# A recurrent attention and soft mixture-of-experts kernel: 24 pieces of unread products on TensorE, and a new table of order

## The chip, the cores and the metric

The kernel runs on one core of a Trainium2 chip. The metric is the time of the program on the device in microseconds (us), as the median of several runs. One run was also recorded by the hardware profiler; the rows below come from that run. The engines are called PE (TensorE: matmuls and transposes), DVE (VectorE), ACT (ScalarE), POOL (GpSimd) and SP (SyncE, which here issues the DMAs). PE's weight loads are listed apart as PEld.

## The reference

The first half is a recurrence over 768 tokens for 4 batches and 8 heads of dimension 40, the second a soft mixture of 8 experts with 4 slots each over its output:

```python
for t in range(S):                                   # S = 768, state is D x D = 40 x 40 per batch and head
    y[:, :, t] = np.einsum('bhd,bhde->bhe', rt, state)
    Sa = np.einsum('bhde,bhe->bhd', state, at)
    state_decay = state * wt[:, :, None, :] - np.einsum('bhd,bhe->bhde', Sa, bt)
    state = state_decay + np.einsum('bhd,bhe->bhde', vt, kt)
...
logits = x @ phi                                     # x: 3072 x 320 (the y of above), 32 slots
d = softmax of logits over the 3072 tokens;  slot_input = d.T @ x
h = np.maximum(slot_input[e] @ w1[e], 0.0);  slot_out[e] = h @ w2[e]     # e of 8, 320 -> 1024 -> 320
c = softmax of logits over the 32 slots;     return c @ slot_out
```

## The kernel before

The recurrence is cut into 12 steps (`st`) of 64 tokens, two to a superstage. Inside a step all tokens are solved at once. `scan_s`, `scan_c` and `scan_k` form running products of the decay on DVE and scale the inputs by them, `bda_at` spreads them, and `gram` multiplies them with each other on PE. `solve_half` (superstage 0) and `solve_step` (the later ones) invert the resulting triangular matrices row by row on DVE and POOL, for a whole superstage; `solve_out` brings the inverse into the layout that PE needs, with a stream transpose on DVE. `ctok_of` and `kbtok` are transposes on PE of scaled inputs.

What runs from step to step is `chain(st)`, in two quarters q of 32 tokens: `chain_v` (products with the values, 32 small matmuls of 32x40), `chain_a` (with the state of before), `chain_e` (a copy), `chain_u` (the nested function `times`: 32 products with the inverse; steps 0 and 1 run it three times, with copies between), and at the end `chain_s`, which forms the new state. `y_ut`, `y_sd`, `y_p` and `y_y` make the output of a step one step later, and `slots` gathers the expert slots. Behind the last step stand `merge_m` and `merge_s` (which bring the partial slots together), the experts' two layers, and 16 output blocks with a DMA each.

All of it is recorded first. Every call of an engine goes through the class `Plan`, which collects operations; an operation is what one stretch of code records for one engine. `emit` then prints them in the order that the string `ORDER` gives (two characters are the number of an operation). The string `ENGINE` chooses DVE or ACT, or DVE or POOL, for each operation that may run on either, and `BANKS` the PSUM bank of each temporary. So each engine's instructions run in the order of the table, and an instruction waits only for what it reads, what it overwrites and its place in its engine's row. The profile gives one line (L509) for all of them, since they are printed by one helper; they are told apart by operation and tile. `cs_t` is the tile of the constants (128x227): `ident`, the unit matrix, its first 128 columns, and some masks. DMAs are all issued by SP in the order of the table.

An f32 matmul call is two matmuls and two weight loads on PE in the trace, a transpose or an f32r matmul one of each.

Of the kernel before, what the change touches and what calls it, by code (L numbers as in the profile page):

```python
# [32 lines left out]


ORDER = (
    "#,#-#/#0#.#2#1#7#4#5#6#3#(#+#&#$#%#9#8#;#:#<#=#@#>#B$R$P#?#D#C#A#'$V#I#H#K#J#G#L#M#F#N$S#E$W$T#e$Q#X#Y#Z#]#["
    "#^#_#P$U#T#g#Q$X#f#O#i#j#`#o#R#n#U$h$_#W#V$e#S$g#h$j$Y$i$`$l#s#m#y#p#q$n$k#{#c$m$o$(#b#k#r$q#a#t#z$#$)#l$*%3"
    "$%$p#d$$$t$M#v#u$N$u$r%2$c$''B$s&O$-$d$x$w$v$&$a&P$.&A$b%5&B$]#w$1$^$f$2$3$Z#}$[&;%4$4%8%7$5&I%6'G#x&C$6$7&J"
    "$+$8$9%9$:%:$;$<%<$,&<%=$y&=%#&E&>%>%-()%;%?$=%@%A%(%,(*$>$?&F%*$0$@${#|$|%&$z%''E%G$A$B$C$D$E$F$G&D$}%0%$$H"
    "$/$I$J$K$L$O%L('%)((%O#*&N%B%F%I%Q%R&Q&R%+&S%%%M&T%/&U%E%C%N&V&Y&W&r&q&s&n&o&p&t&u&w&X%D&Z&y&v&[%K%1&G'=&]'F"  # L40
    "%T&^%H%S%.'@&z&x&{&|%U%V(2%P&_'%'H%W'I%Y%J'#&H&`'D){&a&b%Z&}%[%]%^%_%`%a%b&g)y%c'J&c&e&d'L'$(4'>&f&j&l)|&h'K"
    "&k&m'?'w&i'('M'C's'&''(1'O'P'q(3%d'Q'R(5%e(7'8'S)E%f(6'x)z'.'T'<%X'N%g%h't%i'))@#)'3'r%j':'9%k'/%l'U'W'V%m'A"
    "'Y(9'X'u%n)F'y(<';'Z%o'+'p%p(8'-(U)>%q%r'2%s%t%u%v&K'0'6(;(=+1'v'*+/'[(-(:)A'z'{','1(?'5(@(/(>(++0(F)B'4']'7"
    "(K+2)I'|(P(0(H%w(.'^%x'_%y%z%{%|%}&#&$(,&%(G*((#&&&''}(&(%($&((M(J(O(L)G&)'`(I'a&?)J)H(S*$(N(A'd'e'c'b'f'g&*"
    "*)&+&,'m&-&.&@&/)C*+)<*-&0(Q**&1&2'j(D'h'n(C)D)K'i&3&4&M'k'o)h)j(R'l*,)=)M*Q&5)L&6&7&8&9(B)?(E)n*.)N)i)k)p&:"
    "*&(V(W(X)O(Z)l(T*V)S*P)Q)P&L)T)g)o)R*Z)q)U)r)V)m*0*/*L*4([(](^(_)W*3)}*1)v*'*N*X)s*W*2+e*[+_+b*%*R(`(a(b(c*6"
    "*5*7*=(d(e+`*8+c*S)[)Z)Y(f(g)X)]*#*Y(h(i(j*9(k(l(m)u*?+a+d)^)d)a+f(n*B*>)_*T+g*O*F)e*A)`)b*])f)c*^*_(o(p(q(r"
    "*;)x*C*`*U*a)t)w*<*@*:*y*f+i+h*{(s*E(t(u*D+9+$(v+&+j(w(x(y+k*z*|+^+;*}*c*d*b*e*g,m+3*h*G,i+%*I(z+:+m*M*H({+>"
    "+?+#+<*i+**K+'*l+(*k*j*m,n,k+7,j,l+5*r*n+4+l+,(|(},g)#*u*x)$)%+=+6)&+n+o*o*J,h)'+A)())+8+D+@)*+s+B+E,o+p+C(Y"
    "+G+F+H)+*v+q.R.S*s),)-).*w.T-A-B*t-C-D+S+W+I+).U,e-G+U*p+N*q)/+M+X)0)1)2,f,`,p,b+++t+T)3-K)4)5)6+Z,r+.)7+R,q"  # L50
    "+L-M)8-P-0-8,d+K+P+V+Y+J+O)9):);+z,s-1,w,v,u,t,x-6-2+{+-,y-v+Q+|-E,z-I-w-7-3,{-L+u,c-4-/-N+]-O+[,a-Q-|.#-5-9"
    "-#,},|-$-%-)->-:.$,#,$,%.%,&,',(,),*,+,,-F+r-*-J-=-},-,.-,-x-;-&-H,/-z,0,1/',2,3/*+}-+/----y.X/(/)-<-.-@-'-("
    ".&/+-p/..(/,,4-R//.)-S,5-U.A-V.C-{/1.+.'-W/2-T.-.*-r,6.,.//3../=/4,7,8-q-?/0.I.^,9.G.B,:.D.E.0,;.]/6-s-Y-Z-X"
    ".1.M0/,<.`.O,=.c.H.F-[/5,>.J.Q.2,?.6.Z,@.4.V.b.3.5._,A-t03/7,B-u.a-^.N,C.d,D,E.K00.g-].Y.f-a04.=0501.L,F-c.e"
    ".[.7-`.>.?06-k.W-_02-f.:/<0U.8.@.i,G-l.h.9-m-i07,H,I,J,K,L,M,N0i-o.;-n.<0g.j.k1x0V/8-e.l/>0j-b1y.w/&.P,O,P,Q"
    ",R,S,T,U,V,W,X.m-j09-g0:080;/91:-h.r0+0h.z.|0<0W.p.n0*.t0T/:,Y.q-d.s.v0q,Z,[,].o.y0^0[0s0v,^,_/D.x0=0X0Y/#.}"
    "/E/F/H/I/J.{1F0A0@0>0?0C0B0Z0]1z0o1H.u0k0_/G1@0D1?/K/L/$0.1{/%/M1A0E0r0G0F0t0,0H0`0w1D0m0I1>0a2K1I0d0N1E0Q0p"
    "0J1B2N1=/N2L1G0K2Q1C/O/P/Q2M2O2P1J0l2R/;0-0n2S0b/R2T0u/S0x/T0y0c0f1g/U0z0|0{0L0R/V0O/W1i0M1m5K1#0S0P1K0}1%1L"
    "1h1$150e1M1N2U1o/X/Y/Z/[/]/^1;1j2V1k/_2W/`/a2X2b172(2Z16/b1O1Q1S2'1P1R1T1U2Y/c/d2*1n1&2[181(101V1l2)191p/e/f"
    "1'122+/g2./h2//i1*/j/k142,/l/m1q2a/n1[1)1f1+/o/p/q1<2-2#211r1Z111Y5J1X3Q22201W46131c1]231w262$/r25244,3R1d1e"  # L60
    "3O4.1`1^1_2F3P1|274-4/2<1-2A1}/s/t1a1b3Y/u1.3Z/v/w/x3[2I/y/z/{2c2%1u2H2:2D2?2J2;/|/}1,0#2G2B3W293]1/3U5Y1s28"
    "3S400$0%2&0&0'0(0)3X2i2=2C2@2>1t3x2j2k2m2n2o4#3^3V2p2q3|3}472E3_3b3`3v3y3a3d3c4A42482]5A3w5@3e1v2^3T4{4y3u2_"
    "4G2r2s2t2u2v2w2x3f4B4|3z4I3{2y4z443g3k3i3j3h4C4D5T/@3o3N3r4@4=4$4%4H2z2{2|2}3s3#3t4K3$5D3l3p414&3q4}5h5%435&"
    "5(3m3n3%4L3&3'4M5#4N5B5$4O5C5[5Z4E5E3(494(3)4J4)3*4'4+4h454F4n3+4S5)3,4j3-4R3.4p3/30314P4Q4U4T4V5'325X5*4W33"
    "342l354k365M5G4i375L38393:3;3<5V5F5W4*4l5,4o3=5`3>3?4m3@4q4Y4X4Z4[4d4a4]5b2`4^4e4;5-5.3A4b4g5/3B5c4f4<5U4r5j"
    "5+/?5_506D4c5a3C5d5f3D3E5^4_3F4`3G3H3I3J3K3L3M5g5?5]4:4t4v5l5k5m4u4x635i6-51525n5e6+585s+v+w+x+y4s616B5o6.53"
    "5N625I6,745p5r5q6<2e2f2g2h5t5u575v5S5H54556@5x59/A5R4w6//B5z5y605w5|64/C565;6$656E6%6&6'7?6*666m6C6A6=5}6F6("
    "6j6p6n6k6)6#757A5{6>706l6H6G6q6I5P6o6r6J6L6?6N6M4>68696K675<5O6;5=6X6Z6a6P6O6_6Y4?7,6[6t6:6]6u6Q6v6w7C6s6x6`"
    "6b7=76797:6c7D7G7f6R7B6^6d7W##7@7i6{6W7^7;7m2d6|777-5Q6U6}6e7<6S6g7E7Z6f6i7Q7[7M7>6y7e7R6h6T7k7X7K7H7S7N7L7O"
    "7Y5:6z7$7T7_7U7%7]7`7P7V7u7#7x8(7{7y8)7/7g7&5>7v7w7|7z7}8$8%8#8&7I738-8.7q8'837'7.8K8L7r8/72878*8889848?807p"  # L70
    "818A8>7l828B7c8,718M8C8@8D8E8F8G858I8H8J8N8O8P8Y8Z7d8Q8[8]8j8X8S8W8T8V8U8i6V8k8R8x7(7)7*7+8y788c7s868^8:7j8r"
    "8d7h7a7o7t8;8s7b8_8a8f8l8e8m7n8g8h8b8z8w8t8v8`8u8n8o8p8q9>8<9?9@9A8{8=9B9L9F9R9X8+7F7J9Y9G9I9H9O8|9M9U9C9Z9N"
    "9S9J9K9T9P9Q8}9#9$9V9%9,9W9)9*9D9&9'9E9-9.95929698939/9+999094919(979:9;9<9="
)
# [1163 lines left out]
```

## Time and profile before

| what | value |
|---|---|
| median of 3 runs | 364.82 us (363.41 to 366.78) |
| the profiled run's own time | 365.54 us |
| its span in the trace | 363.7 us |
| PE busy | 322.2 us, 89% of the span, 7425 matmuls |
| DVE busy | 287.4 us, 79% |
| ACT busy | 225.4 us, 62% |
| POOL busy | 115.6 us, 32% |
| mean granted clock of PE | 0.961 |

The profiled run's time is that of the whole program and the span that of what the profiler shows inside it; 1.8 us lie around the span. Busy time is a share over stages with different limits, so the stretches and the chain of waits say more than this table. The granted clock of 1.0 is 2.4 GHz, 0.5 is 1.2 GHz.

### The profile page before, as it was taken

Reading aid. Unit: us, or ns where it says so; the run is one execution under the profiler, and the core shown is the slowest. Engines: PE = TensorE matmul, PEld = TensorE weight load, DVE = VectorE, ACT = ScalarE, POOL = GpSimd, SP = SyncE. Lnnn points to the kernel's source line nnn. Section 1 sums busy time; section 2 is a strip of 40 time slices with the busy share of each in tenths; the row PEclk is TensorE's granted clock in tenths of the full one; section 3 lists DMA queues with packets and bytes.
Section 4 is the critical chain, followed back from the end, with each engine's and each line's share of the span. In section 5 each row is a group of like instructions: output and inputs, shape, how many; then the busy total and the mean of one; then the engine's idle time right before and its main releaser. Section 6 shows DMA issues by size and latency. Waiting matters only on the chain.

```text
span 363.7 us, 16917 instructions
## 1 busy us (share of the span) xinstructions
PE 322.2 (89%) x7425; PEld 281.5 (77%) x7425; DVE 287.4 (79%) x608; ACT 225.4 (62%) x527; POOL 115.6 (32%) x230
## 2 busy tenths in 40 slices
...
GB/s 245 337 248 16 241 14 159 84 51 191 35 172 205 62 77 194 196 87 77 262 104 187 195 99 203 260 205 167 187 235 230 168 295 108 268 313 250 3 192 243
DMA packets 35938, 62.42 MB, mean 172 GB/s; under 512 B 3832, under 2 KB 21368, under 8 KB 35864
## 3 DMA queue, kind: packets, MB, share of 16 engines
...
q8 instruction: 58, 0.95, 1.1%
...
## 4 chain that ended last, share of the span: by engine, by line
PE 72%; DVE 12%; issue 6%; POOL 4%; ACT 2%; DMA 1%; DVEq 0%; ACTq 0%; POOLq 0%
PE ps L509 72%; DVE wt L509 8%; POOL wt L509 4%; DVE ps L509 3%; ACT wt L509 2%; DMA wt<-in_aa_dram 1%; DVE mem L509 1%; ACT mem L509 0%; ACT old_r L509 0%; ACT mid_r L509 0%; DVE slx L509 0%; DVE old L509 0%; POOL mem L509 0%; DVE mlast L509 0%; ACT mid L509 0%
## 5 line engine op out<-in xcount | busy, mean ns | idle before, releaser
L509 PE MATMUL ps<-wt,wt 32*32 32x40 f32 (+7 forms) x2936 | 143.4, 239 | 10.5 <-issue 5.3
L509 PEld LDWEIGHTS ps<-wt,wt 32*32 32x32 f32 (+7 forms) x2936 | 131.1, 133 | 19.5 <-issue 10.2
L509 PE MATMUL ps<-wt,mem 128*64 128x40 f32 (+7 forms) x1088 | 88.0, 295 | 2.7 <-issue 2.3
L509 ACT ACTIVATE wt<-ps 32x320 f32<-32x320 f32 (+1 forms) x181 | 72.8, 402 | 19.6 <-PE ps L509 13.6
L509 PEld LDWEIGHTS ps<-wt,mem 128*32 128x32 f32 (+6 forms) x1088 | 67.3, 123 | 16.0 <-issue 9.8
L509 ACT COPY wt<-ps 32x256 f32<-32x256 f32 (+4 forms) x126 | 55.7, 458 | 18.9 <-PE ps L509 8.6
L509 POOL TENSOR_TENSOR wt<-wt 128x220 f32<-128x220 f32 (+17 forms) x107 | 49.4, 462 | 50.8 <-DVE wt L509 30.2
L509 POOL TENSOR_TENSOR wt<-wt,wt 128x108 f32<-128x108 f32 (+16 forms) x97 | 48.9, 504 | 40.2 <-DVE wt L509 31.9
L509 ACT COPY mem<-ps 128x320 f32<-128x320 f32 (+4 forms) x79 | 32.5, 430 | 46.5 <-PE ps L509 44.0
L509 PE MATMUL ps<-cs_t,wt 120*128 120x120 f32 (+4 forms) x352 | 46.7, 274 | 15.7 <-DMA cs_t<-in_consts_dram 10.0
L509 DVE TENSOR_TENSOR wt<-ps,cs_t 64x512 f32<-64x512 f32 (+1 forms) x74 | 49.3, 677 | 5.1 <-PE ps L509 4.8
L509 PEld LDWEIGHTS ps<-cs_t,wt 120*128 120x128 f32 (+4 forms) x352 | 37.5, 147 | 18.4 <-ACT wt L509 15.8
L509 PE MATMUL ps<-wt 120*64 120x192 f32 (+1 forms) x288 | 47.3, 314 | 0.0
L509 DVE TENSOR_TENSOR_SCAN ps<-wt,wt 128x390 f32<-128x390 f32 x48 | 45.5, 966 | 0.3
L509 PEld LDWEIGHTS ps<-wt 120*64 120x64 f32 (+1 forms) x288 | 36.4, 137 | 0.0
L509 DVE TENSOR_TENSOR wt<-wt,ps 128x384 f32<-128x384 f32 (+1 forms) x48 | 34.4, 740 | 0.6 <-ACT wt L509 0.5
L509 ACT ACTIVATE wt<-wt,bm_t 128x768 f32<-128x768 f32 (+1 forms) x36 | 29.1, 867 | 3.1 <-DVE wt L509 3.1
L509 DVE TENSOR_TENSOR wt<-wt,wt 128x234 f32<-128x234 f32 (+15 forms) x67 | 21.7, 324 | 5.0 <-POOL wt L509 3.6
L509 POOL TENSOR_SCALAR_AFFINE_SELECT wt<-wt 128x1024 f32<-128x1024 f32 x6 | 7.6, 1266 | 56.1 <-DVE wt L509 41.9
L509 DVE STREAM_TRANSPOSE wt<-wt 128x1024 f32<-128x1024 f32 x12 | 24.7, 2081 | 0.7 <-ACT wt L509 0.3
L509 PEld LDWEIGHTS ps<-mem,wt 32*32 32x32 f32 x1792 | 19.4, 108 | 6.3 <-ACT mem L509 3.3
L509 PE MATMUL ps<-mem,wt 32*32 32x40 f32 x1792 | 22.9, 201 | 1.4 <-ACT mem L509 0.5
...
## 6 DMA issues: line engine op xcount, KB each, us to landing
...
```

Of the source, the lines that this page charges most:

```text
L509: eng.dma_start(dst, src)
```

## The change

A new function records 24 pieces. Each is two f32 products of the unit matrix with the whole tile of constants, into a PSUM bank of its own that no operation reads. The tables are replaced by others, in which the pieces have their places. Of the tables one line of each is shown.

```diff
@@ -33,47 +33,48 @@
 ORDER = (
-    "#,#-#/#0#.#2#1#7#4#5#6#3#(#+#&#$#%#9#8#;#:#<#=#@#>#B$R$P#?#D#C#A#'$V#I#H#K#J#G#L#M#F#N$S#E$W$T#e$Q#X#Y#Z#]#["
...
+    "#(#,#-#&#7#1#0#/#.#2#3#5#6#$#%#Q#P#?#S#R#4#T#V#U#Y#W#@#Z#'#B#X#`#8$k#q#]$i#[#a#_#b$m#^$l$o#c$p#}#d#x#r#l$n$q"
...
-ENGINE = "11111111111111111111111111111111111000001100111110100000...
+ENGINE = "11111111111111111111111111111111110000111000000000001000...
-BANKS = "102327013457241654366050002150265737503402171131375156103716...
+BANKS = "700016625067633671105412104336041735637252402551000245602414...
@@ -951,6 +952,16 @@
             load_g(kbr.put(st), kb[st])
             load_g(ahs.put(st), aa[st])
         load(cs_t, consts)
+
+        def keep_busy():
+
+            v = bank("busy")
+            for _ in range(2):
+                nc.tensor.matmul(v[:, 0:227], ident, cs_t, start=True, stop=True)
+
+        for _ in range(24):
+            keep_busy()
+            nc.open = None
         for st in range(2):
             scan_s(st)
             scan_c(st)
```

On PE the number of recorded matmul calls goes from 4011 to 4059. Of the 24 pieces 13 stand ahead of the first product of the recurrence, chain_v(0,0): four at the very start, four behind the Grams of step 0, two behind those of step 1, and three single ones. One stands in `merge_s`, ten behind the last product of the program. Among the operations with a choice, `solve_half` has 8 going from POOL to DVE and 3 the other way, `solve_step` 53 from DVE to POOL and 56 back, `chain_u` 7 of its copies from ACT to DVE and 5 back, the output copies 8 from ACT to DVE and 2 back.

The start of SP's row, where the inputs of the first two steps are loaded. In before:

```order
L509 DMA wt_70<-in_ww_dram 128x782
L509 DMA bm_t<-in_consts_dram 128x3
L509 DMA wt_70<-in_kb_dram 128x768
L509 DMA wt_74<-in_aa_dram 128x384
L509 DMA wt_70<-in_kb_dram 128x768
L509 DMA wt_70<-in_ww_dram 128x782
L509 DMA wt_74<-in_aa_dram 128x384
L509 DMA cs_t<-in_consts_dram 128x227
```

In the change:

```order
L942 DMA wt_70<-in_ww_dram 128x782
L942 DMA bm_t<-in_consts_dram 128x3
L942 DMA cs_t<-in_consts_dram 128x227
L942 DMA wt_74<-in_aa_dram 128x384 x2
L942 DMA wt_70<-in_kb_dram 128x768 x2
L942 DMA wt_70<-in_ww_dram 128x782
```

The constants have moved from the eighth place to the third; the first kb load has two aa loads and the constants ahead of it instead of none.

PE, at the end of step 0's chain, from the last `times` (mem, wt_74) of quarter 1 to the state products of `chain_s` (wt_76 with wt_75); cs_t with mid is the transposes of `y_ut(0,1)`, wt_76 with wt_71, wt_72 and wt_74 is `chain_v(1,0)`, eight times the same three rows. In before:

```order
L509 MATMUL ps_62<-mem,wt_74 32x40 x32
L509 MATMUL ps_61<-cs_t,wt_73 128x120 x2
L509 MATMUL ps_61<-cs_t,wt_73 128x80
L509 MATMUL ps_63<-cs_t,mid 120x128 x3
L509 MATMUL ps_65<-wt_76,wt_71 32x40
...
L509 MATMUL ps_68<-wt_76,wt_75 120x120 x4
L509 MATMUL ps_62<-wt_76,wt_75 80x80 x4
L509 MATMUL ps_64<-wt_76,wt_75 120x120 x4
```

In the change:

```order
L942 MATMUL ps_67<-mem,wt_74 32x40 x32
L942 MATMUL ps_66<-cs_t,wt_73 128x120 x2
L942 MATMUL ps_66<-cs_t,wt_73 128x80
...
L942 MATMUL ps_68<-wt_76,wt_75 120x120 x4
L942 MATMUL ps_67<-wt_76,wt_75 80x80 x4
L942 MATMUL ps_62<-wt_76,wt_75 120x120 x4
L942 MATMUL ps_61<-cs_t,mid 120x128 x3
L942 MATMUL ps_65<-wt_76,wt_71 32x40
```

The state products have moved ahead of `y_ut(0,1)` and `chain_v(1,0)`.

PE in step 8, quarter 1, from the last products of `chain_v` (wt_76 with wt_71) to `times` (mem, wt_74); the rows between are transposes for the output, for `kbtok` and for `ctok_of`. In before:

```order
L509 MATMUL ps_61<-wt_76,wt_71 32x40 x2
L509 MATMUL ps_66<-cs_t,mid 120x128 x3
L509 MATMUL ps_67<-cs_t,wt_70 128x120 x4
L509 MATMUL ps_64<-cs_t,mem 128x128
L509 MATMUL ps_68<-cs_t,wt_73 128x120 x2
L509 MATMUL ps_68<-cs_t,wt_73 128x80
L509 MATMUL ps_62<-cs_t,wt_73 128x120 x2
L509 MATMUL ps_62<-cs_t,wt_73 128x80
L509 MATMUL ps_61<-cs_t,wt_76 120x120 x4
L509 MATMUL ps_64<-mem,wt_74 32x40 x32
```

In the change:

```order
L942 MATMUL ps_64<-wt_76,wt_71 32x40 x2
L942 MATMUL ps_65<-cs_t,mem 128x128
L942 MATMUL ps_63<-cs_t,mid 120x128 x3
L942 MATMUL ps_66<-cs_t,wt_70 128x80 x4
L942 MATMUL ps_61<-mem,wt_74 32x40 x32
L942 MATMUL ps_64<-cs_t,wt_70 128x120 x4
```

Fewer transposes stand between the two groups of small products.

## Rows read from the trace of the kernel before

**Rows 1.** The page's list of engines: busy us (share), matmuls or instructions.

```profile
PE 322.2 (89%) x7425; PEld 281.5 (77%) x7425; DVE 287.4 (79%) x608; ACT 225.4 (62%) x527; POOL 115.6 (32%) x230
```

**Rows 2.** Stretches: busy us per engine (count), granted clock, DMA share, GB/s.

```profile
0.00:10.00 10.00, 0.00 (x0) 0.02 (x1) 6.30 (x12) 2.24 (x3) 3.65 (x7) 1.00 0.78 259
20.00:30.00 10.00, 4.71 (x34) 4.36 (x33) 9.98 (x16) 9.68 (x25) 0.00 (x0) 0.92 0.55 181
...
50.00:60.00 10.00, 6.99 (x272) 5.66 (x272) 9.82 (x16) 7.93 (x20) 0.99 (x1) 0.79 0.46 143
...
70.00:80.00 10.00, 10.00 (x305) 8.99 (x296) 9.83 (x22) 7.20 (x19) 4.26 (x9) 1.00 0.21 56
```

**Rows 3.** Chain of waits: start, us, what; behind x, matmuls.

```profile
98.81 2.12 DVE wt L509
...
101.06 50.57 PE ps L509 x1336
...
234.93 3.40 PE ps L509 x127
238.33 1.07 issue
239.40 4.56 PE ps L509 x127
243.96 1.57 issue
```

**Rows 4.** Stretches at half the granted clock, same columns.

```profile
52.40:55.80 3.40, 3.40 (x102) 2.58 (x93) 3.30 (x6) 2.79 (x8) 0.00 (x0) 0.50 0.35 80
...
59.20:66.10 6.90, 5.31 (x85) 4.76 (x86) 2.85 (x8) 4.89 (x9) 3.74 (x9) 0.51 0.07 25
...
247.00:250.40 3.40, 3.40 (x25) 3.26 (x25) 1.25 (x4) 0.48 (x1) 0.54 (x1) 0.51 0.33 119
```

**Rows 5.** Timeline of PE, 10 to 40: start, us, operation, wait ahead.

```profile
10.01 3.03 PE L509 MATMUL ps<-cs_t,wt 120*128 120x120 f32 x14 [10.01 <-DMA cs_t<-in_consts_dram]
14.53 2.04 PE L509 MATMUL ps<-wt,wt 120*128 120x192 f32 x6 [1.48 <-ACT wt L509]
...
21.50 3.76 PE L509 MATMUL ps<-wt,wt 120*128 120x192 f32 x24 [0.82 <-ACT wt L509]
...
36.70 1.15 PE L509 MATMUL ps<-wt,wt 120*128 120x192 f32 x6 [0.41 <-ACT wt L509]
```

**Rows 6.** PE's waits from 62 to 360: total us, times, longest.

```profile
PE ps L509 <- issue: 8.7, 9, 1.6
```

**Rows 7.** The page's list of DMA queues: packets, MB, share.

```profile
q8 instruction: 58, 0.95, 1.1%
```

**Rows 8.** Timeline of DVE, 0 to 13 and 56 to 69.

```profile
8.87 2.73 DVE L509 TENSOR_TENSOR wt<-wt,ps 128x384 f32<-128x384 f32 x4
...
61.68 0.25 DVE L509 TENSOR_TENSOR wt<-wt 128x84 f32<-128x84 f32 x1 [1.31 <-POOL wt L509]
...
65.06 0.66 DVE L509 TENSOR_TENSOR wt<-ps,mem 120x480 f32<-120x480 f32 x1 [2.32 <-PE ps L509]
```

**Rows 9.** Timeline of PE, 56 to 69.

```profile
57.49 0.50 PE L509 MATMUL ps<-cs_t,wt 120*128 120x120 f32 x3 [1.05 <-ACT wt L509]
57.92 0.79 PE L509 MATMUL ps<-mem,wt 32*32 32x40 f32 x64
...
62.52 4.47 PE L509 MATMUL ps<-wt,wt 32*32 32x40 f32 x47 [1.32 <-issue]
```

**Rows 10.** Timeline of PE, the last matmul.

```profile
355.86 0.27 PE L509 MATMUL ps<-mid_r,mid_r 128*128 128x160 f32 x1
```

**Rows 11.** Timeline of SyncE, from 353.

```profile
354.88 4.82 SPq L509 DMA_DIRECT2D out_dram<-wt  x7
```

**Rows 12.** SyncE's waits, from 340: total us, times, longest.

```profile
SPq L1234 <- DMA out_dram<-wt: 2.9, 1, 2.9
```

More of the change, by code (lines that the diff above doesn't have):

```diff
@@ L35 @@
 ORDER = (
-    "#,#-#/#0#.#2#1#7#4#5#6#3#(#+#&#$#%#9#8#;#:#<#=#@#>#B$R$P#?#D#C#A#'$V#I#H#K#J#G#L#M#F#N$S#E$W$T#e$Q#X#Y#Z#]#["
[L37 to L70, printed above, removed]
@@ L76 @@
-BANKS = "102327013457241654366050002150265737503402171131375156103716576670522421452065361244107267553310451473165617605137503720671732071540316753612143041312053071203434532545632740110555017116264555664270243574170570701510252036710267336013643321513170435504770253352577404346014552556227605501331264612371653340752506303513552261461555075044510755166173436347747124523744344711215606351262517751262657304033277532524547652271574457175442564125463077277243105"
+    "#(#,#-#&#7#1#0#/#.#2#3#5#6#$#%#Q#P#?#S#R#4#T#V#U#Y#W#@#Z#'#B#X#`#8$k#q#]$i#[#a#_#b$m#^$l$o#c$p#}#d#x#r#l$n$q"
@@ new lines @@
+    "$$#e#t$&#f#i$j#|$'#y#g$r$,#h'/#A#j#m$+$#$(#o#s%'%%$/#k%&#p#{%($-$*%)#=$%#n#u#D%*$.#>%,$0%-$1#z#v$)$2$;%.%+$?"
+    "$w$=$<$@%0%2$6$x$B%/$3$7$}$8#9$A%1#*$:#+%J%K$E$F$I$J#;$K$u'0$v%L${$L$|%#%O$5$M$s#:$t$>%3%4%M%P$y$z&[&S&T$D$4"
+    "%5#C%N&Y&U&b&^%6$C&Z$N',$G$O%;&]%Q$f&_%$$P%R$Q&c$R%E%T$g&V%>%V&`#<%U(A#w&h$S%S$T$U$V$W&g%:$X$Y$Z$[$]$^%7%8#)"
+    "%Y%@&a%X%W%e%=(B$_$`$a%<$9$H$b$c$d'^%A'.%?%B'-$e$h%I%`%a%j&i%l%Z%9&j%i%c&k&l%g%G&m'Y%D%F%[(=&n&q&o&r&p&t%f&u"
+    "%b'X%d&s&v&w'[%k%C'2&x%H'a'7'4%^%]&y'1'3&z'5%h'9'='U'8':';'V%_&}'W'#&|%o%p&{'<'$*8*6*7(?%r''(@')'_'%'c'+'6(I"
@@ new lines @@
+    "(N'b%m'e'(%n'*'&'f'd'Z(4(0'h'i(.']*9'>'?'j'@'k(6%s%t%u%v'l'm'o'r'n%w%x%y%z%{%|%}'p(K&#(J'P'F##'Q&$(O&%'`&&(1"
+    "&''A(L(-(M&((/(2(:'q(5&)&*(Q&+(;&,&-&.&/(P&0'g'J's'T'G&1&2&3&4(R(U&5&6'D'H(T(7(3&7'K(C'B(S(G'C(E'E'S'O%q't(W"
+    "(>(X(V'R(8(n(F'u'N)^(d(H)`(D(_'M'L'v'w&8(f)U)_&W'x)a'y(Y'I&X)T(9(i&9&:&;&<&=*@(<)Y&>&?&@&A*B(b)b)V*E(e'|'z'}"
+    "'{(*&B&C(h(#)Z(Z(g&e&f&D*A&E)c)[)](+('(a&F&G&H(k&I($&J&K&L&M&N&O&P&Q&R(m*C(,(](`(c*F(((l)d*'*%([(%(&()*+*-(^"
+    ")f*&)e+G+I)g(j(o)h*(*)*<+J)X+H*D)m*k*>)l(p)k(q)i)j)n*,*.*/*l)o*H)p(s*e*G)W*L*:*K*I*=*o*0*$(t*q**+}+z*N*O*M(u"
@@ new lines @@
+    "*J*;+w*p)t*U)q)s)u)r(v(w(x(y(z&d({(|*s+{+x*P(})#)$)%)&*m*5*2+y*?*1*g*n+|*4*u,#,$)|*t*r*S)'+Q*h)y*Z*j*T*R,&,%"
+    ")(*X,',(*Q)v*i)}*W*_)z*#))*Y)*)+),){)w)-)x*3+8+6*v*x+S,**w*[*y).*{*z*}*|+#)/)0+9*f+V*]*V+<+>+$,)+M*`,++K+%+7"
+    ")1)2+:*^*b)3+R+v)4,0)5)6+=+&+W*a+T+U+X)7+Z+?+@*d+[+*,})8)9+;+)+'+():+Y+5);++*c)<+]+O,{+A,1)=+,)>+B+D+F+C+E+`"
+    "+2-#+^-(+/,|+_-))?)@.k)A)B)C+P)D)E+N+3+0+L+4-*+a.l-,)F)G-&-'-Y-Z-[-]+b-$.m+g+-+f.n+l+.+1)H---.-+)I-d-%-P-H-/"
+    "-G)J,x)K+p)L+h)M)N)O+m+q+e+d+i+c.;+k-f(r-i)P)Q)R)S,7-0+n+j+r+o+s,y,8,9,;-2,<-J-N-4-K-1-3-5-6-7,,.3-O,--`,.,="
@@ new lines @@
+    "-8,>,:,?-^-I+u.9.4+t-L-e-9-<-;-=-:,@,z,/-A,A-g-j-h,B-Q,C,D,E-M-D-R.=-B,F-C->-a-S/E/?-E-_.7.<.:/B.5/@,G/A/C,H"
+    ",I,J-F-?-@.>.?,K/D,L/F/G.1.--l.8.@-p.v-k.A-b0F,M.6/I/J/K/H/P/L-m,N,O/Q-c-o/N/R-X-U-T-V.[.].Y.Z-W.b.`.x.^./.E"
+    ".C.B.F.D.G-n-r/U/M-s-q/O.(,P,Q,R,S.H.u.s-t,T.w.y,U.2.{-v._0G0H...X.),V0K-x.z.I,W.0.a,X.c,Y,Z,[-u.K.M.J.|.d-y"
+    ".L,].N-w.e.o/#,^0L,_.t,`,a/$0O.p.U.}0P,b/>.q,c.r.R/%.,.#/&-{.O.V0I.S.+25.T0E/)0M,d-}.*.W1(0Q,e,f,g,h.P.Q/T0J"
+    ",i,j,k,l,m.i.h.f.g.j,n0R/(/',o1W0N//.%/0/3/90T,p,q,r,s,t,u,v,w26/*/4.&-|/1/V/2.'/./50n-z/-0p/,/8/+0t.$/]0U/;"
@@ new lines @@
+    "0S/60o0q0r0v/:0W0X0Z/^0u1&0s/_0V0Y1$0[/a/=/b0w0x0D1'1/110B1.1%100]12/c/d0^/e1)1*/f/</g1,0y0m/71+2g2d/h0_1]0b"
+    "0`0a0c2h0C1-141U2j1V0j1X2e0d1^1Z2f2i130k0l1Y/i/j/k/l1[1c2k2l27/m1_16150g,219/n1R/o1:/p2n1`/S172o2p/q1#0{0|0z"
+    "2&2$/r0}2q280e1;5c2*180f0h4N0i1d1e/s/t1<1=2m1f/u/v1g/`1i1l2r1a1b1M2,1O2%2'1N1k1h2(1T1j1m/w2?1Q1>/x2A/y2+2s1n"
+    "2t/z1B/{2@1H1?/|2B2C/}292)0#2-1P2.1@2G0$2F0%2K0&0'2z1A1o2J1L0(0)2I1J2/1S1I2D2#2E3r2H2y2{0*0+1C561K57214F2=1r"
+    "1p1s1q0,0-0.0/00010203042:05060708090:581x1t2;4G4D202L1F2M0;0<2<1{1y591z1u1|4E1v5d3n2N2>1G1E3o2O1}2T2Y2_3p2P"
@@ new lines @@
+    "1w1D2Q3h243j2R3s2V2b2[223q3i3t2a3k5Y452]2W3u4;0=2^0>0?2Z0@0A3&23432`3v2S2U3'492c2X3x3w444H3l3z3y3{4P3|2u5r4O"
+    "5o4Y4:4L463(5m3)3*3+3}4#3,5X4U3-4Z3.3g3/4(3m4&4'4J4%4$2v2w4`30313233343536374[38474)484<4]424/2x4,5n4d4*4041"
+    "4=4-4+394.4e4g3:3;3<3=4I3>4>5@5:4h5;4M5=4^4b5]3?3@3A3B3C3D3E5<5>5^4f4l5Z5t5[4K5w5s4A4?4@5?4C5%4c5'4Q4i4k4j3F"
+    "3G3H3I3J3K3L4X4n5&5e4o5+3M5-4_4p5A3N3O5B4m5q5x4u5(5z6%5_5,3P4S3Q5f5$3R5D4t6'5`4B4a5)3S3T3U3V3W3X3Y3Z4r/W4s3["
+    "4q4v5{5E4y5*5F4R5G4T4|3]5y5H3^3_3`3a3b3c5.5/5g5p5v5u4w6&4z5P51534{525C556K6E5I4}5#4x6(6)3d3e3f5W5J5O6*6+6I5Q"
```

15 lines of the change are left out of this document (11 added, 4 removed).

## The prediction

> **What bounds the kernel now.** I read the page first, then the stretches of ten microseconds, the chain of waits, PE's own waits, and last the timelines of the start and the end. All sums are made against the profiled execution: a span of 363.7 us and a time of 365.54 us, which is 0.7 us above the median of the three runs (364.82).
>
> PE is busy in 89% of the span [rows 1]. The stretches say where it is the bound. From 50 to 60 DVE is busy for 9.82 of 10 us and PE for 6.99: the prologue belongs to DVE. From 70 to 80 PE is full (10.00) with DVE close behind (9.83) [rows 2]. The chain of waits agrees: at 98.81 a DVE transpose of 2.12 us releases 50.57 us of PE without a break [rows 3]. So the two engines are tied together at each superstage's inverse ("solve_out"), and a change must shorten both, or one of these hand-overs.
>
> Two losses of PE can be seen. The first is its clock. In 52.4 to 55.8, 59.2 to 66.1 and 247 to 250.4 the granted clock is 0.50 or 0.51, the lower of its two levels (1.2 of 2.4 GHz) [rows 4]; a second late stretch, from 274.3 to 277.7, is like that from 247. At the start the page's clock row is no witness: six Gram products last 2.04 us at 14.53 and 1.15 us at 36.70, so the start too runs low [rows 5].
>
> The second is "issue": PE waits for nothing that the profile shows, 8.7 us in 9 pieces from 62 on [rows 6]. In the chain such pieces stand behind groups of exactly 127 matmuls (3.40 us, then 1.07 lost; 4.56, then 1.57) [rows 3]. The queue for instructions brought 58 packets, 0.95 MB, or 16.4 KB each [rows 7]; PE's 7425 matmuls and as many weight loads are 14,850 instructions, 256 to a packet, so a packet is 128 matmuls. I read it so: where PE runs through one block too quickly, the next isn't there yet.
>
> **The change, part by part.**
>
> *The pieces.* A piece is two f32 products of 227 columns, four passes over PE. 24 Gram matmuls (4096 columns) take 3.76 us at 21.50 [rows 5], so 0.92 ns a column, and 908 columns cost 0.83 us; at the low clock about 1.6 (2.04/1.15 times as much gives 1.5, and the transposes from 10.01, 3.03 us for 1600 columns, give 1.7).
>
> Four pieces stand first: 6 to 7 us at the low clock. They need only the constants, whose load moves from the eighth DMA to the third. In the first 10 us the queue moved 259 GB/s [rows 2], so the 0.51 MB up to it take 2.0 us, and with as much for the start of the queue they land near 4 us, and the pieces end between 10 and 13. PE's first real work started at 10.01, released by these constants, and its next at 14.53 waited for ACT [rows 5]. The chain from 10 to 14 is DVE and ACT, not PE. Cost 0; without ACT's lag it would be up to 2.5 us of PE, which DVE's prologue still covers. The loads that the constants pass (a kb half, 0.49 MB later) would land about 1.5 us later, near 6.5, and their first product on DVE starts at 8.87 [rows 8]: 0.
>
> The other nine pieces of the prologue (7.5 us at full clock, 15 at low) lie behind the Grams of st 0 and 1. PE idles 5.29 of the 10 us from 20 [rows 2], the largest hole; at the low clock the pieces fill it and what smaller ones there are. Cost between 0 and 1 us.
>
> *The end of the prologue.* Before, PE runs y_ut(0,1) and the 32 products of chain_v(1,0) ahead of the state products chain_s0; there it loses 1.32 us to issue, and 4.47 us pass over the next group of 32x40 products and the state products recorded with it [rows 9]. DVE waits 2.32 us there, until 65.06 [rows 8]. The change puts the state products first. They can come some 2 us earlier; but DVE's work ahead of the first inverse is the same to 0.2 us, and DVE waited 1.31 for POOL just before [rows 8]. I take a gain of a third, 0.7, with bounds of -2.0 (the whole) and +1.0 (the fillers delay a Gram).
>
> *The blocks.* Behind 62 us PE's work stands in nearly the same order (no landmark moves by more than some 4 us of work, and DVE's sum ahead of the inverses by -1.5 to +2.9 us), but cut otherwise into 256s. I summed PE's full-clock time in each block by the order and the lengths in the trace. Before, four blocks hold under 3.35 us of work (3.32, 2.99, 2.94, 2.58), and the stops behind three of them are 0.61, 1.07 [rows 3] and 0.77: 2.45 over four, 0.6 each. After, eight are so short, three of them near 2.1 us, because chain_v(st,1) and "times" of the same step now meet in a block. In step 8 they bring 60 of its calls, or 120 of 128 matmuls; 64 such matmuls take 0.79 us [rows 9], so 1.5 us, and the transposes between them bring it to 2.1. Four more at 0.6 are 2.4 us; I take half, 1.2, since several end where the chain of one quarter waits for copies anyway. Bounds: 0 (all there), and 5.6 (each costs 1.0, worked out below).
>
> The Trainium skill ("Runtime: NRT & Kernel Launch", section "Instruction fetch mechanics") describes instruction memory as refilled in 16 KiB blocks of 256 instructions, and says that this is hidden by the pace of issue. The size agrees with the 16.4 KB here; the hiding doesn't, with 8.7 us of stops. By that rule this term is 0 and the sum 0.5 above before.
>
> *The merge.* One piece, 0.83 us, between two products, where PE has a wait for DVE's small steps. 0, at most 0.8.
>
> *The tail.* Ten pieces stand behind the last product, which ended at 356.13 (355.86 + 0.27) [rows 10]. Ten are 8.3 us by the Grams, so PE ends at 364.4. Before, the last outputs left SyncE's queue in the 4.82 us from 354.88 [rows 11], to 359.70; with 2.9 us of waiting for their landing [rows 12] that is 362.6, and 1.1 us of closing steps lead to 363.7. PE becomes the last. Bounds: 0 (its columns pass a tenth quicker than the Grams', and the closing steps don't follow it) and 1.8 (364.4 and the closing steps, 365.5). I take 1.2, nearer the upper end, since the closing steps have to stand behind every engine. At the low clock it would be some 8 more, which I leave to the slower case, as PE doesn't idle ahead of it.
>
> *Copies between engines* (10 output copies, 12 of chain_u, solve steps 53 to POOL, 56 from it): equal in number both ways; ±1, taken as 0.
>
> Sum: -0.7 + 1.2 + 1.2 = +1.7, so 367.2 against 365.5; less 0.7 for the profiled run, **366.5 us**.
>
> **Rivals.** One per cent here is 3.6 us: 361.2 to 368.5 is no change.
>
> *Faster, 359.6.* If PE is occupied in the prologue, the clock is high when the chain of st 0 comes, and the low stretches go. 59.2 to 66.1 holds 5.31 us of PE at 0.51: 2.6 us too many, 2.3 of it on the path; the two late stretches hold 3.40 each, 1.7 too many each [rows 4]. -2.3 - 3.4 - 0.7 + 1.2 = -5.2: 360.3, less 0.7. For it: the waits ahead of low stretches are there to be filled. Against: the pieces stand behind the Grams and ahead of chain_v(0,0), none behind the first "times", where waits as that of 1.05 us at 57.49 stand [rows 9]; none before 247 or 274. The Trainium skill ("TensorE: Matmul & The Clock Gate", "Why this matters for your kernels") advises to leave no long idle gap between bursts, which is this rival; the trace agrees in that the low stretch from 59.2 follows such a wait, the 1.05 us at 57.49 [rows 9]. By the rule alone I would say faster.
>
> *Slower, 370.9.* A block stops PE by what it lacks of 3.35 us. The four of before lack 1.6 together and cost 2.45; the eight of after (3.31, 2.08, 3.25, 2.56, 3.02, 2.08, 2.94, 2.18) lack 5.4, which in proportion is 8.3; at 1.0 each I take 8.0, +5.6, and -0.7 + 5.6 + 1.2 = +6.1: 371.6, less 0.7. It decides if a stop costs above 0.75 on average. For it: 1.57 and 1.07 have been seen [rows 3]. Against: a block of 2.99 cost nothing before.
>
> *The pieces and the cuts do nothing, 364.8.* PE's stops stay where the chain waits anyway, its end isn't waited for, DVE's own work holds the prologue: every term is 0.
>
> Chances: forecast 0.28, nothing 0.12, faster 0.27 and another 0.05 for gains of the new order that I don't see, slower 0.24 and another 0.04 for a late clock or fillers that delay a Gram. So faster by over 1% 0.32, within 1% 0.40, slower 0.28. Signs are mixed, so the range is wide: 358.5 (faster, a good microsecond below its price) to 372.5 (the slower case with the upper bound of the tail). The forecast's own is 363.5 to 369.
>
> **What would show it.** PE's "issue" from 62 on: near 10 us for the forecast, 14 for the slower case, under 9 for "nothing". The granted clock in 52 to 66: still 0.5 for the forecast, 1.0 for the faster case. PE's last instruction near 364 and behind the last output's landing. DVE's wait ahead of the state products below 2.3 us, and the first "times" of st 2 less than 1 us earlier than 101.06. I am wrong if solve_out(0) moves by more than 2 us or if the low stretches late in the span go.

## The result

The change runs in 368.45 us (median of 20 runs, 365.53 to 374.33) against 364.63 us before (20 runs, 359.18 to 370.16): 3.8 us more by the medians. The ratio is 1.0146, with a 95% interval of 1.0112 to 1.0181. That is slower by over 1%, which had a chance of 0.28; it is inside the forecast's range, between its point (366.5) and its slower rival (370.9).

Runs of these two kernels spread over 9 and 11 us. Ratios and their intervals leave out runs more than 1.5% above the fastest of their kernel, in some sets most of before's, so medians and differences below are of all runs. Before was run again with each set of experiments: 364.14 us with e1 to e4, 364.11 with e5 to e8, 365.31 with e9 to e11. The change's profiled run took 366.61 us; only three of its 20 runs are lower, so its trace shows less of the loss than a typical run has. Its span is 364.9 us.

The page and PE's waits, which answer to [rows 1], [rows 7] and [rows 6]:

```profile
PE 335.3 (92%) x7521; PEld 295.4 (81%) x7521; DVE 295.1 (81%) x622; ACT 222.6 (61%) x521; POOL 112.6 (31%) x222
...
q8 instruction: 59, 0.97, 1.1%
```

```profile
PE ps L942 <- issue: 10.0, 10, 2.6
```

PE is busier by 13.1 us, which is less than the 22.5 us of the pieces: the other products took 9 us less, at least in part by the clock (the first Grams, below). The stops rise from 8.7 to 10.0 us behind 62; ahead of it they rise more, as the chain of waits shows (start, us, what; answers to [rows 3]):

```profile
55.69 2.44 issue
58.13 3.25 PE ps L942 x123
...
250.28 4.16 PE ps L942 x128
254.44 1.48 issue
...
264.55 3.96 PE ps L942 x126
268.50 2.61 issue
271.11 15.47 PE ps L942 x379
```

The stop at 55.69 stands inside one `times` of step 0. Stops of 0.3 us and more sum to 13.8 us over the whole span, 8.7 before. Again they come behind 126 to 128 matmuls, but for one of 0.58 us at 45.92, which stands ahead of the same product wherever the cuts fall. And something follows a stop that I had read past in the rows of before: the clock. The stretches at half (answer to [rows 4]):

```profile
50.50:64.00 13.50, 8.96 (x270) 7.49 (x271) 9.80 (x13) 7.32 (x20) 2.45 (x6) 0.50 0.39 88
...
272.30:275.70 3.40, 3.40 (x23) 3.15 (x23) 2.92 (x7) 0.19 (x1) 0.63 (x3) 0.50 0.40 111
```

The stop of 2.61 us ends at 271.11, and from 272.3 on PE runs at half for 3.40 us. In before the stop of 1.57 from 243.96 [rows 3] stands ahead of the low stretch from 247 [rows 4] in the same way. So a long stop can be paid twice. It is not always: behind the 1.48 us from 254.44 the clock stayed full.

The start and the end of PE (timeline: start, us, operation, wait ahead; answers to [rows 5] and [rows 10]) and SyncE's last waits (to [rows 12]):

```profile
4.78 5.64 PE L942 MATMUL ps<-cs_t 128*128 128x227 f32 x16 [4.78 <-DMA cs_t<-in_consts_dram]
...
13.13 2.00 PE L942 MATMUL ps<-wt,wt 120*128 120x192 f32 x12 [0.90 <-ACT wt L942]
...
17.04 3.38 PE L942 MATMUL ps<-cs_t 128*128 128x227 f32 x16
...
355.81 0.49 PE L942 MATMUL ps<-mid_r,old_r 128*128 128x160 f32 x3
356.14 7.87 PE L942 MATMUL ps<-cs_t 128*128 128x227 f32 x40
```

```profile
SPq L1245 <- DMA out_dram<-wt: 2.7, 1, 2.7
...
SPq L1245 <- PE ps L942: 0.2, 1, 0.2
```

The first four pieces last 5.64 us; the first twelve of their 16 products stand 0.38 us apart, the rest 0.19, so three quarters of them run at the low clock. The Grams behind them take 2.00 us for twelve matmuls, in before 2.04 for six [rows 5]. The last ten pieces end at 364.01 and SyncE waits 0.2 us for them behind the last output.

### The profile page after: what moved, and what is told of

Same layout as the page of the kernel before. It is cut to its first block, busy times and chain, and to the rows that moved or that the text cites. A ratio compares the mean times of both kernels' runs of the same rounds, so it can differ in the third digit from the quotient of the medians.

```text
span 364.9 us, 17101 instructions
## 1 busy us (share of the span) xinstructions
PE 335.3 (92%) x7521; PEld 295.4 (81%) x7521; DVE 295.1 (81%) x622; ACT 222.6 (61%) x521; POOL 112.6 (31%) x222
## 4 chain that ended last, share of the span: by engine, by line
PE 79%; DVE 7%; ACT 5%; issue 5%; DMA 2%; POOL 1%; DVEq 0%; SPq 0%; ACTq 0%; POOLq 0%
PE ps L942 79%; ACT wt L942 4%; DVE wt L942 4%; DVE ps L942 3%; DMA wt<-in_vv_dram 1%; DMA wt<-in_aa_dram 1%; POOL wt L942 1%; DVE mem L942 0%; ACT mem L942 0%; ACT mid_r L942 0%; ACT old_r L942 0%; DVE slx L942 0%; DVE old L942 0%; ACT mid L942 0%; ACT old L942 0%
## 5 line engine op out<-in xcount | busy, mean ns | idle before, releaser
L942 PE MATMUL ps<-wt,wt 96*32 96x40 f32 (+7 forms) x2936 | 138.5, 234 | 6.7 <-ACT wt L942 5.2
L942 PEld LDWEIGHTS ps<-wt,wt 96*32 96x32 f32 (+7 forms) x2936 | 126.7, 129 | 17.2 <-issue 7.8
L942 PE MATMUL ps<-wt,mem 128*64 128x40 f32 (+7 forms) x1088 | 86.0, 294 | 2.8 <-issue 2.6
L942 ACT ACTIVATE wt<-ps 32x256 f32<-32x256 f32 (+1 forms) x181 | 72.7, 402 | 15.9 <-PE ps L942 12.7
L942 ACT COPY wt<-ps 32x256 f32<-32x256 f32 (+4 forms) x121 | 53.2, 458 | 23.2 <-PE ps L942 12.4
L942 POOL TENSOR_TENSOR wt<-wt,wt 128x84 f32<-128x84 f32 (+16 forms) x98 | 49.2, 502 | 55.6 <-DVE wt L942 31.4
L942 POOL TENSOR_TENSOR wt<-wt 128x30 f32<-128x30 f32 (+17 forms) x98 | 46.2, 472 | 38.8 <-DVE wt L942 22.0
L942 PE MATMUL ps<-cs_t,wt 120*128 120x120 f32 (+4 forms) x352 | 44.7, 262 | 2.9 <-issue 1.6
L942 PE MATMUL ps<-cs_t 128*128 128x227 f32 x96 | 22.5, 389 | 4.9 <-DMA cs_t<-in_consts_dram 4.8
L942 DVE TENSOR_TENSOR wt<-wt 128x168 f32<-128x168 f32 (+16 forms) x66 | 22.3, 338 | 2.9 <-POOL wt L942 1.5
```

The source lines that it names most:

```text
L942: nc.gpsimd.memset(t, 0.0)
```

## The experiments

In these, *lack* is a number that the order and the matmuls' lengths in the trace give: over all blocks of 256 instructions of PE behind the prologue, the sum of what each has less than 3.55 us of work (the forecast's 3.35 and the 0.2 that its stops were longer than the shortfall). Before has 2.4 us, the change 7.4. It is worked out, not read from a view: blocks as they ran in the traces, with a few records missing, give about 7 us in the change and only about 6 in e4 (10.4 below). Of the 24 pieces the 13 in the prologue put 104 instructions ahead of the recurrence, and so they move every later cut.

**The order without the pieces (e1).**

```diff
             for o in order:
+                if o.who == "keep_busy":
+                    continue
```

> The change's order, engines and banks, with the 24 pieces left out (nothing of the reference is missing). Lack is the sum, over PE's blocks of 256 instructions behind the prologue, of what each is short of 3.55 us of work: 2.4 us for before, 7.4 for the change, about 2.9 here, since 104 instructions fewer stand ahead of the recurrence. Theory A (the cost is the cuts of the instruction blocks, and the tail): 364 to 366 us, near before, and the issue stops of PE fall from 13.8 us to 8 or 9. Rival B (the new order and the new engines of the copies cost): 367 to 369, as the change. Rival C (the pieces earn something by PE's clock, which the order needs): 369 to 372, with the granted clock at half in the prologue.

Measured: 364.38 us, ratio 1.0024 to before (0.9982 to 1.0066). The new order and the new engines cost nothing by themselves, as theory A has it; but rival C's sign is there too. The clock is at half in the prologue, and the Grams take (timeline of PE):

```profile
13.13 3.22 PE L944 MATMUL ps<-wt,wt 120*128 120x192 f32 x12
...
22.65 3.58 PE L944 MATMUL ps<-wt,wt 120*128 120x192 f32 x12 [4.22 <-DVE wt L944]
```

against 2.00 for the first twelve of the change; and the first inverse is transposed 3.7 us later than in the change (DVE's timeline: e1, the change, and before):

```profile
46.60 2.13 DVE L944 STREAM_TRANSPOSE wt<-wt 128x1024 f32<-128x1024 f32 x1
```

```profile
42.87 2.12 DVE L942 STREAM_TRANSPOSE wt<-wt 128x1024 f32<-128x1024 f32 x1
```

```profile
44.20 2.12 DVE L509 STREAM_TRANSPOSE wt<-wt 128x1024 f32<-128x1024 f32 x1
```

So the pieces do earn something in this order, and something else takes it away.

**The pieces cut to one element (e2).**

```diff
-                nc.tensor.matmul(v[:, 0:227], ident, cs_t, start=True, stop=True)
+                nc.tensor.matmul(v[0:1, 0:1], ident[0:1, 0:1], cs_t[0:1, 0:1], start=True, stop=True)
```

> The change with every piece cut to one element: as many instructions at the same places, next to no work. The cuts are those of the change (lack 7.4 us). Theory A: the stops stay, only the tail's ten pieces go, so 367 to 368.5 us (the change's 368.45 less 0 to 1.2). Rival B2 (what costs is PE's time in the pieces, 22 us of it): 364 to 366, as with no pieces. Rival C (the pieces earn by the clock): 370 or more, the clock at half in more of the prologue than with the full pieces.

Measured: 371.03 us (6 runs), ratio 1.0196 (1.0135 to 1.0257). The instructions without the work are worse than the change, by 2.6 us (0.0 to 5.2), though the tail is gone. PE's time in the pieces isn't the cost (rival B2 falls); theory A alone gave 367 to 368.5 and is off on the side of rival C.

**The change with its cuts moved (e3).** 38 products of one element, 152 instructions, stand at the start of PE, where it waits for DMAs. 104 + 152 is one block of 256, so the recurrence is cut as with no pieces.

```diff
-FILLS = {}
+FILLS = {28: (38, 2, 3)}
...
-            self.nc.tensor.matmul(bank, src, src, start=True, stop=True)
+            self.nc.tensor.matmul(bank[0:1, 0:1], src[0:1, 0:1], src[0:1, 0:1], start=True, stop=True)
...
+        nc.idle += (bm_t,)
```

(An entry of `FILLS` is the operation ahead of which the products are issued, their number, the bank, and which tile they read; tile 3 is the small constant that is loaded second.)

> The change with 38 products of one element more (152 instructions) at the very start of PE, where it waits for inputs: all later cuts fall where they fall without the pieces (104 + 152 = 256), lack 3.1 us in place of 7.4; the pieces and their work stay. Theory A: 364 to 366 us, 3 to 4 below the change, the stops at 9 or 10 us. Rivals B and B2 (order or work of the pieces): 368.4, as the change; the 152 instructions would only add a little.

Measured: 360.82 us, 7.6 us below the change (95% of the resampled differences of medians lie between 4.8 and 9.6; later brackets behind a difference are the same). The first inverse comes at 42.86, as in the change, so the added products leave the prologue as it was. Against before the medians differ by 3.3 us (0.5 to 4.9), but the ratio is 0.9995 (0.9939 to 1.0051): whether e3 beats before is unclear. Theory A is right in its sign and too small: 3 to 4 us were expected. PE's stops behind 62 (answers to [rows 6]):

```profile
PE ps L942 <- issue: 4.5, 8, 1.1
```

and in this trace no clock below full is left behind 64.

**Before, cut at its worst (e4), at its best (e6), and a whole block on (e9).** The same edit on before, with 22, 54 and 64 products; the line is e4's.

```diff
-FILLS = {}
+FILLS = {137: (22, 4, 3)}
```

> The kernel before with 22 products of one element (88 instructions) at the very start of PE: nothing but the cuts changes, lack 10.4 us in place of 2.4. Theory A: slower by 4 to 8 us, 369 to 373, the stops at 13 to 17 us in place of 8.7. Rival (the stops come when the DMA queues are loaded, wherever the cuts fall): 364.6, no change, stops as before.

Measured for e4: 374.68 us (6 runs), ratio 1.0317 (1.0241 to 1.0392): 10.5 us more (7.7 to 14.5; 4 to 8 were expected) for 88 instructions that last about a microsecond in an idle engine.

> The kernel before with 54 products of one element (216 instructions) at the very start of PE: lack 0.5 us in place of 2.4, the least of all shifts. If each us of lack costs about 1.3 us, as the 10 us of e4 for 8 say: 361.6 to 362.6 us, 2 to 3 below before. Rival: a shift can only hurt, since what is left of stops comes from loaded DMA queues: 364, no change. Rival: any instructions at PE's start cost (e4's 10 us were that): slower than before.

Measured for e6: 360.44 us, ratio 0.9915 (0.9877 to 0.9953), 3.7 us less than before and a microsecond below the expected range.

> The kernel before with 64 products of one element (256 instructions, one whole block) at the very start of PE: every later cut falls where it fell before. If e4 and e6 came from the cuts: 364.1 us, as before (within 1). If the 1 x 1 products themselves help or hurt (by waking PE early, or by taking time): 361 to 362 or lower, or 366 and more.

Measured for e9: 364.15 us. By the medians that is 1.2 us less than before in its set (from 2.0 less to 1.6 more), by the ratio of 1.0056 (1.0007 to 1.0104) 2 us more. Neither is near the 10.5 and 3.7 us of e4 and e6: the products themselves do little, and where they put the cuts decides. The rivals named in e4 and e6 fall as causes of these differences. PE's stops in e4, e6 and e9:

```profile
PE ps L509 <- issue: 9.8, 10, 1.6
```

```profile
PE ps L509 <- issue: 4.3, 4, 2.0
```

```profile
PE ps L509 <- issue: 7.4, 8, 1.9
```

e4's 9.8 is less than the 13 to 17 expected; but its trace is of the fastest of its six runs (370.92). The chain of waits of that run shows a stop where before had none, and the windows show the clock that follows:

```profile
161.26 1.45 issue
162.71 7.47 PE ps L509 x99
```

```profile
163.50:166.90 3.40, 3.40 (x21) 3.40 (x20) 1.68 (x4) 0.48 (x1) 0.59 (x2) 0.52 0.23 63
```

**The tail.** e7 is the change without its last ten pieces, e5 the same with e3's cuts.

```diff
+                if o.n in (34, 35, 36, 37, 39, 40, 41, 42, 43, 44):
+                    continue
```

> The change without the ten pieces behind the last product; all cuts and all else as in the change. If PE's end sets the program's end: 367.3 to 368.0 us (0.4 to 1.2 less than the change's 368.45). If the last output's landing does: 368.4.

> The change with the 152 instructions at the start, as in e3, and without the ten pieces behind the last product. If PE's end sets the end of the program (the forecast's term, +1.2, bounds 0 and 1.8): 359.5 to 360.5 us, e3 less 0.4 to 1.2. Rival: the landing of the last output sets it, PE's pieces run beside it: as e3, 360.8.

Measured: e7 367.15 us (1.0057, 1.0012 to 1.0103), e5 360.13 us (0.9955, 0.9913 to 0.9997): 1.3 and 0.7 us less than with the pieces, both inside the spread of the medians (-3.9 to +0.5, and -3.2 to +2.2). The traces measure it better. From the end of the last real product to the end of the span e7 has 360.8 - 353.28 = 7.5 us (its last row below), before has 363.7 - 356.13 = 7.6, and the change 364.9 - 356.30 = 8.6. The tail costs 1.0 us.

```profile
352.78 0.50 PE L944 MATMUL ps<-mid_r,old_r 128*128 128x160 f32 x3
```

**Which pieces earn (e8).** As e5, but the nine pieces behind the Grams, and the one in the merge, are one element wide.

```diff
-        def keep_busy():
-
+        def keep_busy(i):
+            n, w = (128, 227) if i in (0, 7, 8, 10) else (1, 1)
             v = bank("busy")
             for _ in range(2):
-                nc.tensor.matmul(v[:, 0:227], ident, cs_t, start=True, stop=True)
+                nc.tensor.matmul(v[0:n, 0:w], ident[0:n, 0:n], cs_t[0:n, 0:w], start=True, stop=True)
```

> As e5 (152 instructions at the start, no tail), but of the 14 other pieces only the four at PE's very start are whole; the nine behind the Grams and the one in the merge are cut to one element, with the cuts unchanged. If the gain of the pieces (e3 stands 3.6 us below e1, with like cuts) is earned at the start, where PE's clock is low when the first Grams come: as e5, about 360.3, with the first inverse ending near 45. If the nine in the gaps of 17 to 40 earn it: 362 to 364, with the clock at half somewhere in 20 to 40 and the first inverse at 46 to 48.

Measured: 364.69 us, ratio 0.9983 (0.992 to 1.0047), 4.6 us above e5 (1.6 to 5.4): even a little over the second case. By the median the first four alone are worth nothing (e1 has 364.38). The clock falls in the gap behind the Grams (half from 20.7 to 27.5), and the first inverse comes 2.5 us later than in e5 (DVE's timeline, e8 and then e5):

```profile
45.39 2.08 DVE L944 STREAM_TRANSPOSE wt<-wt 128x1024 f32<-128x1024 f32 x1
```

```profile
42.85 2.06 DVE L944 STREAM_TRANSPOSE wt<-wt 128x1024 f32<-128x1024 f32 x1
```

These 2.5 us are earned by the nine in the gaps from 17 to 38. The other 2 arise later and are not separated: e8's trace is also at half from 324.4 to 327.9, in the merge, whose piece is narrow here, and its stops behind 68 are 2.2 us longer than e5's.

**Pieces in before's order (e10).** 13 pieces, the constants loaded third, and the cuts of e6.

```diff
+PIECES = {137: 4, 149: 4, 153: 3, 151: 1, 308: 1}
+FILLS = {137: (28, 4, 3)}
...
+        cs, bm = self.ops[20], next(o for o in order if o.eng == "SP" and o.dma == 128 * 3 * 4)
+        order.remove(cs)
+        order.insert(order.index(bm) + 1, cs)
...
+                if o.n in PIECES:
+                    at_line(self.idle[2], self.piece, (PIECES[o.n], self.banks[list(o.banks)[0].place][:, 0:227]), {})
```

> The order of before with 13 whole pieces in the prologue, four at PE's start, four behind the Grams of step 0, three behind those of step 1, two single ones, the constants loaded third as in the change, and 28 products of one element, so that 104 + 112 = 216 instructions stand ahead and the cuts are those of e6. If the pieces' gain (3.6 us in the change's order, e3 against e1) is a gain in any order: 357 to 359 us, the first inverse ending near 44.9 in place of 46.4. If it only repays what the change's order loses without them (first inverse 48.7 in e1, 46.3 in before): 360.4, as e6.

Measured: 367.32 us, ratio 1.0058 (1.001 to 1.0107), 6.9 us above e6 (4.6 to 10.7), of which 1.2 is the difference of before between the two sets: neither case. The timeline of PE shows why (L280 is the line of the pieces here):

```profile
29.91 4.91 PE L280 MATMUL ps<-cs_t 128*128 128x227 f32 x12 [4.43 <-ACT wt L519]
34.61 0.74 PE L519 MATMUL ps<-cs_t,wt 120*128 120x120 f32 x3
35.28 0.91 PE L519 MATMUL ps<-wt,wt 32*32 32x40 f32 x64
```

I gave the pieces the bank of the operation behind them, so three of them waited 4.43 us for the same copy that it waited for. They filled no gap; the clock fell in it, and then the three at the low clock, 4.91 us, stood ahead of the transposes. DVE is busy for 0.78 of the 5 us from 35, and the first inverse comes at 48.57, against 44.35 in e6. The experiment doesn't say what well-placed pieces would do for before's order; it says that a piece needs a bank that is already free, which the change's table of banks gives it.

**Pieces in the chain of step 0 (e11).** Five of the tail's pieces, each ahead of a `times` or of `chain_v(0,1)`, in a bank free there; the other five are left out, and the cuts are e5's.

```diff
+MOVE = {34: (342, 6), 42: (350, 6), 36: (352, 1), 37: (354, 1), 44: (356, 1)}
+FILLS = {28: (28, 2, 3)}
...
+        for n, (t, p) in MOVE.items():
+            order.remove(self.ops[n])
+            order.insert(order.index(self.ops[t]), self.ops[n])
+            list(self.ops[n].banks)[0].place = p
...
+                if o.n in (35, 39, 40, 41, 43):
+                    continue
```

> As e5 (cuts as there), but five of the ten pieces from the tail stand in the chain of step 0, each in a wait of 0.5 to 1 us ahead of a times or of chain_v(0,1). The forecast's faster rival: PE's clock stays high from 50 to 64, where it is at half for 13.7 us in e3 and e5: 2 to 4 us less than e5, 356 to 358. The other side: at the low clock a piece lasts 1.6 us in a wait of 0.6, the clock falls all the same, and each delays the chain: 362 to 365.

Measured: 364.90 us, ratio 0.9978 (0.9925 to 1.0032), 4.8 us above e5 (1.4 to 5.6), of which 1.2 is again the difference of before between the sets: the other side of what was expected. PE's timeline, in the slowest of its 12 runs (367.56):

```profile
54.10 1.88 PE L949 MATMUL ps<-cs_t 128*128 128x227 f32 x4 [1.82 <-ACT mid L949]
55.91 0.34 PE L949 MATMUL ps<-mem,wt 32*32 32x40 f32 x4
57.62 1.28 PE L949 MATMUL ps<-mem,wt 32*32 32x40 f32 x60 [1.37 <-issue]
58.83 1.88 PE L949 MATMUL ps<-cs_t 128*128 128x227 f32 x4
```

A piece lasts 1.88 us at the low clock, and the stop of 1.37 us is still there. The stretch at half is shorter than in e5 (windows, e11 and then e5):

```profile
53.80:64.00 10.20, 8.53 (x143) 6.48 (x143) 0.00 (x0) 2.23 (x6) 0.00 (x0) 0.50 0.18 58
```

```profile
52.10:65.80 13.70, 10.58 (x278) 9.11 (x279) 10.39 (x14) 8.37 (x22) 3.64 (x9) 0.50 0.43 96
```

The granted clock, as a median of all runs, is 0.979 against e5's 0.970. So these pieces raise the clock a little, and the time that they stand in the chain costs more than that gives back.

All together, ordered by cuts:

| kernel | lack, us | median, us |
|---|---|---|
| before's order, 216 instructions ahead (e6) | 0.5 | 360.44 |
| before's order | 2.4 | 364.63 |
| before's order, 256 ahead (e9) | 2.4 | 364.15 |
| before's order, 88 ahead (e4) | 10.4 | 374.68 |
| change's order, no pieces (e1) | 2.9 | 364.38 |
| change, 152 ahead (e3) | 3.1 | 360.82 |
| change | 7.4 | 368.45 |
| change, pieces of one element (e2) | 7.4 | 371.03 |

In each pair that differs by the cuts, with before of the same set, a microsecond of lack is 1.3 to 1.9 us of time: (374.68 - 364.14) / 8.0 = 1.3, (364.11 - 360.44) / 1.9 = 1.9, (368.45 - 360.82) / 4.3 = 1.8, (371.03 - 364.38) / 4.5 = 1.5.

The granted clock of every run is on record, and it moves with the cuts. Its median is 0.968 in the change and 0.981 in e3; what is missing to 1, times the median, is 12.0 us and 6.9. In e4 it is 0.949 and in before of its set 0.962: 19.1 and 13.8 us. As an estimate, for a PE that is always busy, the clock is some 5 of the 7.6 us between the change and e3, and some 5 of the 10.5 between e4 and before.

e5 (360.13) and e6 (360.44) beat both kernels; e6 by adding nothing but 216 instructions to before.

## Why the prediction was right or wrong

**The whole.** The sign and the range held. The forecast was +1.7 on the profiled run, and 1.1 was measured (366.61 against 365.54); on the median 366.5 is +1.9, and 3.8 was measured. That the sum came this near is in part luck: the cuts cost some 6 us more than its term for them, and the pieces of the prologue, to which it gave a cost of 0 to 1, gave back several us.

**The blocks: the right mechanism in part, mis-sized.** The term was +1.2, "four more at 0.6 are 2.4 us; I take half", with bounds 0 and 5.6. e3 against the change measures the cuts by themselves: 7.6 us of median (4.8 to 9.6), for 4.3 us of lack. Three things were wrong.

Halving was: of the eight blocks listed as short six stopped PE in the change, for 4.8 us together (the one of step 8, with 2.3 us of work, for 0.55), against 2.45 us behind the short blocks of before, so the whole 2.4 was there.

The reading "where PE runs through one block too quickly" covers only part of the stops, and the price of 0.6 was taken from that part; no row shows its limit of 3.35 us. Behind a block of 4.56 us PE stopped for 1.57 [rows 3], and in the chain of before one stop stands behind 127 matmuls that took 5.78:

```profile
265.55 5.78 PE ps L509 x127
271.33 1.23 issue
```

In the change 5.2 of the 10.0 us of stops behind 62 stand behind blocks of more than 3.55 us, the longest (2.61) among them; in before it is 4.9 of 8.7.

And a stop was priced by its own length, where some are followed by PE at half clock (161.26 in e4, 268.50 in the change). By the estimate above the clock is the greater part of what the cuts cost between e3 and the change. Which stretches hold it is not shown: the traces of the change and of e4 are of runs below their medians.

The Trainium skill ("Runtime: NRT & Kernel Launch", section "Instruction fetch mechanics") has the fetching of blocks hidden behind the pace of issue. By that rule e4, e6 and e9 would take the same time; they measured 374.68, 360.44 and 364.15 us.

**The prologue: near the right size for the wrong reason.** The term was -0.7; the transpose of the second inverse begins 1.1 us earlier (97.72 against 98.81 [rows 3]). The forecast gave this to the state products that move ahead, and gave the pieces a cost of 0 to 1. The state products did little: DVE's first step on them begins at 64.75 in place of 65.06 [rows 8]. The pieces were worth 3.6 us by the median (e3 against e1, 0.5 to 5.5) and 3.7 by the first inverse, and the new order without them was 2.4 us late there (46.60 against 44.20). The step that failed is "the prologue belongs to DVE", from which a faster PE was worth nothing there: in e1, with PE at half clock, DVE is busy for 26.5 of the 30 us from 10, in the change for 29.6.

**The tail: right.** +1.2 was forecast, 1.0 measured, and the pieces ended at 364.01 for 364.4.

**The faster rival: half right.** Its place was wrong, as argued: the chain of step 0 stays at half, 13.5 us from 50.5, and in e11 pieces there shorten this and still cost time. Its mechanism was real one stage earlier, from 17 to 40. The slower rival came nearest to the size of the cuts (+5.6 for 7.6) and lacked the pieces' gain. From e1, which takes before's time, -3.6 for the pieces with their tail and +7.6 for the cuts make +4.0; 3.8 was measured.

**What was named to watch.** Stops near 10 us behind 62: 10.0. Clock still at half from 52: yes. PE ending near 364: yes. DVE's wait ahead of the state products below 2.3: 0.43. The first `times` of step 2 less than 1 us earlier: 1.03, just missed. Of the two signs of being wrong, solve_out(0) moved by 1.3 us, inside the 2; but no late low stretch was to go, and one of the two went, that at 247, with the stop ahead of it. The one of 274 came at 272.3, behind a stop of its own.
